# Gated linear attention and routed experts: squares summed on the matrix engine, masks ahead of key copies, and a re-timed instruction order

## The chip, the cores and the metric

The kernel runs on one core of a Trainium2 chip. A core has engines that run side by side, each through a queue of its own: TensorE multiplies matrices (PE in the profile; PEld is its loading of weights), VectorE (DVE) and ScalarE (ACT) work element by element, GpSimd (POOL) and SyncE (SP) mostly issue transfers here. TensorE writes into PSUM, eight banks of 512 fp32 columns on 128 partitions; the other data lie in SBUF. The metric is the time of one execution on the device, in microseconds.

## What is computed

The reference has two stages. The first is an attention with a complex gate per key dimension; the gate's size is limited to 0.999 first:

```python
B, H, S, D = 4, 8, 768, 48
mag = np.sqrt(a_re * a_re + a_im * a_im)
scale = np.minimum(mag, 0.999) / (mag + 1e-06)
a_re_n, a_im_n = (a_re * scale, a_im * scale)
for t in range(S):
    new_re = ar * S_re - ai * S_im          # ar, ai: gates of step t
    new_im = ar * S_im + ai * S_re
    kv = np.einsum('bhd,bhe->bhde', k[:, :, t], v[:, :, t])
    S_re, S_im = (new_re + kv, new_im)
    y[:, :, t] = np.einsum('bhd,bhde->bhe', q[:, :, t], S_re)
```

Its output, 3072 rows of 384, goes into eight experts. Each row takes the expert with the largest logit:

```python
logits = x @ w_gate                          # (3072, 8)
expert_idx = np.argmax(logits, axis=1)       # gate_w: softmax weight of that expert
xe = x[mask]                                 # rows of expert e
h = np.maximum(xe @ w1[e], 0.0)              # 384 -> 1024
out[mask] = gate_w[mask, None] * (h @ w2[e]) # 1024 -> 384
```

## The kernel before

The recurrence is written as a product of gates. For each of the four batches the kernel goes through these steps:

- **limit**: the gates of 16 steps lie in four tiles of 4 steps by 144 columns (576 columns of 128 partitions each, real and imaginary). Each is scaled by a function of the sum of its squares.
- **front** and **fix**: running complex products of gates, on VectorE.
- **fold**: the running products are multiplied into the queries, and their inverses into the keys. The inverse needs a sum of squares again, of 768 columns. Transfers then bring the rows into tiles KX and QX of one head each.
- **attention**: for each chunk of 128 steps and each pair of heads: score product, causal mask, output product, and the state that is carried on.

The batches overlap. Every step is recorded as an operation with an engine, a duration and a latency. A scheduler in the kernel itself orders the list by these guessed times, and then each engine's instructions are issued in that order. [...]

```python
def dve(cols, emit, after=(), free=(), first=5):
    return op("V", cols / 960 + 0.068, cols / 960 + 0.19, emit, after, free, first)
def act(cols, emit, after=(), free=(), first=5, n=1):
    return op("A", n * 0.08 + cols / 1200, n * 0.08 + cols / 1200 + 0.15, emit, after, free, first)
def pe(passes, emit, after=(), free=(), first=5):
    return op("T", passes * 0.111, passes * 0.111 + 0.21, emit, after, free, first)
def dma(late, emit, after=(), free=()):
    return op("S", 0.62, late, emit, after, free)
...
for o in in_time(ops):       # the scheduler's order
    o.emit()
```

The limit, with the sum of squares on VectorE (vstt is a three-operand instruction, vtt a two-operand one):

```python
sq = act(2 * n, ... A.activation(sq2, g[:, :, 1:3, :], func=ACT.Square))          # 1152 columns
o = dve(n, ... vstt(s, sq2[:, :, 0, :], 1e-12, sq2[:, :, 1, :], ALU.max, ALU.add), [sq])
ln = act(n, ... A.activation(l, s, func=ACT.Ln), [o])
ex = act(n, ... A.activation(l, l, func=ACT.Exp, scale=-0.5), [ln])
uu = act(n, ... A.activation(u, l, func=ACT.Square, accum_out=good[...]), [ex])
o = dve(n, ... vtt(s, s, u, ALU.mult), [uu])
o = dve(n, ... vstt(l, s, -3.0, l, ALU.add, ALU.mult), [o])
uu = act(n, ... A.activation(u, l, func=ACT.Identity, scale=..., bias=w_bias), [o])
sc = dve(n, ... vstt(s, l, -2 / 0.999, u, ALU.max, ALU.mult), [uu])
o = dve(2 * n, ... )                                                              # gates times s
```

Attention. The diagonals hold the end of a chunk on the diagonal of a matrix, so that a score product yields the state's decay as well; two ScalarE instructions make one for a head and a chunk:

```python
ats = [... for p in ps[0:4]]                    # score banks, used in turn
for c in range(C - 1):
    for i in range(n):
        def diagonal(i=i, c=c):
            for w in range(2):
                A.activation(QX[i][0:R2, c, 128 + w * D:...], diag[:, w, :], func=ACT.Copy,
                             scale=KX[i][0:R2, c * CW + 128 + w:...])
        turn[c, i] = act(96, diagonal, of(kd[i], c), ...)
for c in range(C):
    for j, r in enumerate(units):               # a unit is a pair of heads
        o = pe(6.8 if c < C - 1 else 4, score, ...)                # 4 products of 224 columns
        needs = [dve(256, ... vtt(ak[:, :, 0:128], at[:, :, 0:128], causal, ALU.mult), [o], ak_readers, first=0)]
        if c < C - 1:
            needs.append(act(2 * R2, ... A.copy(ak[:, :, 128:], at[:, :, 128:128 + R2]), [o], ak_readers, first=1))
        o = pe(..., outputs, needs + ...)
        e = act(wide, ... ys from the output bank ..., [o])
        ...                                     # two transposes, state copy, row copy, logits
```

The experts run when all rows have been scattered by expert in DRAM. Their products take turns over three sets of banks:

```python
own = {"x": (6, 7), "h": (2, 3, 4, 5), "o": (0, 1)}[kind]
```

Of the kernel before, what the change touches and what calls it, by code (L numbers as in the profile page):

```python
# [9 lines left out]
FP32 = mybir.dt.float32  # L10
# [127 lines left out]
def gateloop_then_moe(ctx, tc, q, k, a_re, a_im, v, wg, w1, w2, out):  # L138
# [58 lines left out]
    w_bias = consts.tile([128, 1], FP32, name="w_bias")  # L197
    nc.vector.memset(w_bias, -0.4995)
# [60 lines left out]
    ps = [bank.tile([128, 512], FP32, name=f"bank{i}") for i in range(8)]  # L259

    with ExitStack() as att:
# [15 lines left out]
        lsq, fsq = part(1, JQ, 2, NC), part(1, BL, 2, C * NB)  # L277
# [31 lines left out]
        ats = [p.rearrange("p (h w) -> p h w", w=256) for p in ps[0:4]]  # L309
# [11 lines left out]
        def op(engine, busy, late, emit, after=(), free=(), first=0):  # L321
            ops.append(Op(engine, busy, late, emit, list(after), list(free), first))
            return ops[-1]
# [7 lines left out]
        def pe(passes, emit, after=(), free=(), first=5):  # L331
            return op("T", passes * 0.111, passes * 0.111 + 0.21, emit, after, free, first)

        def dma(late, emit, after=(), free=()):
            return op("S", 0.62, late, emit, after, free)
# [20 lines left out]
        def load_gates(b, tiles):  # L356
            cs = columns(tiles)
            for i in range(BL // JQ):
                js = slice(i * JQ, i * JQ + JQ)
                old = sum((state.pop(("gate", i, t), []) for t in tiles), [])  # L360
                raw = [dma(7.5, lambda p=p, src=src, i=i, js=js: Q.dma_start(gates[i][:, :, p, cs], src[b, :, js, cs]),
                           free=old) for p, src in ((1, a_re), (2, a_im))]
                for t in tiles:
                    state["raw", i, t] = raw

        def limit(b, tiles):

            cs = columns(tiles)
            wide = len(tiles) * TC
            for i in range(BL // JQ):  # L370
                w, readers = ring("lim", 2)
                s, l, u = (x[:, :, cs] for x in lim[w])
                g = gates[i][:, :, :, cs]
                sq2 = lsq[:, :, :, cs]
                n = JQ * wide
                sum_at = NG + b * (BL // JQ) + i
                sq = act(2 * n, lambda g=g, sq2=sq2: A.activation(sq2, g[:, :, 1:3, :], func=ACT.Square), state["raw", i, tiles[0]],
                         state.get("lsq", []))
                o = dve(n, lambda s=s, sq2=sq2: vstt(s, sq2[:, :, 0, :], 1e-12, sq2[:, :, 1, :], ALU.max, ALU.add), [sq], readers)
                state["lsq"] = [o]  # L380
                ln = act(n, lambda s=s, l=l: A.activation(l, s, func=ACT.Ln), [o], readers)
                ex = act(n, lambda l=l: A.activation(l, l, func=ACT.Exp, scale=-0.5), [ln])
                uu = act(n, lambda l=l, u=u, at=sum_at: A.activation(u, l, func=ACT.Square, accum_out=good[:, at:at + 1]), [ex], readers)
                state.setdefault("good", []).append(uu)

                o = dve(n, lambda s=s, u=u: vtt(s, s, u, ALU.mult), [uu])
                o = dve(n, lambda s=s, l=l: vstt(l, s, -3.0, l, ALU.add, ALU.mult), [o])
                uu = act(n, lambda l=l, u=u: A.activation(u, l, func=ACT.Identity, scale=-0.5e-6 * 0.4995, bias=w_bias), [o])
                sc = dve(n, lambda s=s, l=l, u=u: vstt(s, l, -2 / 0.999, u, ALU.max, ALU.mult), [uu])
                o = dve(2 * n, lambda g=g, s=s: vtt(g[:, :, 1:3, :], g[:, :, 1:3, :], bc(s[:, :, None, :], [128, JQ, 2, wide]), ALU.mult),  # L390
                        [sc])
                taken_by(readers, o)
                m = act(n, lambda g=g: A.activation(g[:, :, 0, :], g[:, :, 2, :], func=ACT.Copy, scale=-1.0), [o])
                for t in tiles:
                    state["scaled", i, t] = [o, m]

        def front(b, tiles):
# [6 lines left out]
            for j in range(1, BL):  # L404
                g, r = gates[j // JQ], j % JQ
                w = j % 2
                z = zs[w][:, :, :, 0:n]
                at = dims(g[:, r - 1], 2 * NC + cs.start, (-NC, 2), (0, 2), (1, n)) if j == 1 else                     dims(X[:, j - 1], NC + cs.start, (-NC, 2), (0, 2), (1, n))
                m = dve(4 * n, lambda z=z, g=g, r=r, at=at: vtt(z, dims(g[:, r], cs.start, (NC, 2), (NC, 2), (1, n)), at, ALU.mult),
                        state["scaled", j // JQ, tiles[0]] + [o], state.get(("z", w), []))  # L410
                if j == 1:
                    c0 = act(2 * n, lambda g=g: A.copy(X[:, 0, :, cs], g[:, 0, 1:3, cs]), state["scaled", 0, tiles[0]], old)
                o = dve(2 * n, lambda z=z, j=j: vtt(X[:, j, :, cs], z[:, 0], z[:, 1], ALU.add), [m], old)
                state["z", w] = [o]
                steps.append(o)
                for t in tiles:
                    state.setdefault(("gate", j // JQ, t), []).extend([m, c0] if j == 1 else [m])
# [63 lines left out]
        def fold_chunks(b, t, chunks, fixed, lq, lk, packed, free, old, new):  # L481
# [6 lines left out]
            f2, s, l = fsq[:, :, :, at], fs[:, :, at], fl[:, :, at]  # L488
            by_chunk = lambda ap: ap.rearrange("p j (c n) -> p c j n", n=NB)
# [5 lines left out]
            sq = act(2 * n, lambda: A.activation(f2, x, func=ACT.Square), there, old["fsq"])  # L495
            o = dve(n, lambda: vstt(s, f2[:, :, 0, :], LEAST / 1e8, f2[:, :, 1, :], ALU.max, ALU.add), [sq], old["fs"])
            state["fsq"].append(o)

            ln = act(n, lambda: A.activation(l, s, func=ACT.Ln), [o], old["fl"])
# [4 lines left out]
                                                     in0=s[:, BL - 1].rearrange("p (n b) -> p n b", b=NB)[:, :, NB - 1],  # L504
# [10 lines left out]
            o = dve(n, lambda: vtt(s, s, l, ALU.mult), [ex], [g])  # L515
# [20 lines left out]
        def attention(b, g):  # L536
# [16 lines left out]
            for c in range(C - 1):  # L553
                for i in range(n):
                    def diagonal(i=i, c=c):
                        for w in range(2):
                            A.activation(QX[i][0:R2, c, 128 + w * D:128 + w * D + D], diag[:, w, :], func=ACT.Copy,
                                         scale=KX[i][0:R2, c * CW + 128 + w:c * CW + 129 + w])
                    turn[c, i] = act(96, diagonal, of(kd[i], c), state.get(("head", slots[i]), []), first=2, n=4.6)
            st = [None for _ in units]  # L560
            for c in range(C):
                wide = 128 + (R2 if c < C - 1 else 0)
                for j, r in enumerate(units):
                    (w, readers), (wa, ak_readers), (wy, y_readers), (ws, s_readers) = ring("at", 4), ring("ak", 3), ring("yst", 4), ring("ys", 3)
# [8 lines left out]
                    o = pe(6.8 if c < C - 1 else 4, score, sum((of(qd[i], c) + of(kd[i], c) + [turn.get((c, i))] for i in r), []), readers,  # L573
# [3 lines left out]
                    if c < C - 1:  # L577
                        needs.append(act(2 * R2, lambda at=at, ak=ak: A.copy(ak[:, :, 128:], at[:, :, 128:128 + R2]), [o], ak_readers, first=1))
# [9 lines left out]
                    o = pe((4.2 if c == 0 else 7.6) * wide / 224, outputs, needs + [state["vb"][c]] + ([old[1]] if old else []), y_readers,  # L588
# [13 lines left out]
                    if c < C - 1:  # L602
                        (wp, p_readers), (wt, t_readers) = ring("st_ps", 2), ring("st", 4)
                        o = pe(1, lambda wp=wp, ys=ys: T.transpose(st_ps[wp][0:R2, :], ys[:, 128:128 + R2], ident), [e], p_readers, first=rank)
# [6 lines left out]
                    o = pe(1, lambda wp=wp, ys=ys: T.transpose(y_ps[wp], ys[:, 0:128], ident), [e], p_readers, first=rank)  # L611
# [7 lines left out]
                    o = pe(2, lambda c=c, ys=ys, pair=pair: T.matmul(lg_ps[b % 2][:, c, :, pair], lhsT=ys[:, 0:128], rhs=wgate[:, pair, :],  # L619
# [93 lines left out]
        limited = [((0, 1, 2),)] * 4  # L713
        multiplied = [((0, 1, 2),)] * 3 + [((0, 1), (2,))]
        pieces = lambda b, t: ((0, 3), (3, C)) if (b, t) == (B - 1, G - 1) else ((0, C),)
        for b in range(B):
            for tiles in limited[b]:
                load_gates(b, tiles)
            to_limit = list(limited[b])
            for tiles in multiplied[b]:  # L720
                while to_limit and to_limit[0][0] <= tiles[-1]:
                    limit(b, to_limit.pop(0))
# [11 lines left out]
                for t, f in zip(tiles, fixed):  # L734
                    fold(b, t, f)
                    attention(b, t)

# [17 lines left out]
    with ExitStack() as ms:  # L755
# [33 lines left out]
        def bank_of(kind):  # L789
            own = {"x": (6, 7), "h": (2, 3, 4, 5), "o": (0, 1)}[kind]  # L790
            turn[kind] = turn.get(kind, -1) + 1
            return ps[own[turn[kind] % len(own)]]
# [273 lines left out]
```

## Time and profile before

| what | value |
|---|---|
| time, median of three runs | 695.32 us (694.79 to 696.25) |
| span of the profiled execution | 693.6 us |
| TensorE busy | 518.6 us (75%) |
| VectorE busy | 373.5 us (54%) |
| ScalarE busy | 295.5 us (43%) |
| mean granted TensorE clock | 0.93 |

Most of the kernel's instructions are issued by one helper, so nearly all groups carry its line, L134; they are told apart by operation, by the tiles that they write and read, and by shape. "out<-in" names these tiles, without buffer numbers: "big" are the large buffers that hold gates, squares and running products in the attention and the weights in the expert stage, "ak" is the masked score tile, "bank" is PSUM. Behind the bar stand the group's busy time in us, the mean ns of one instruction, and the idle time of the engine just before them with what ended it. In a timeline the columns are the start in us, the duration, the engine, the instruction, how many in a row, and in brackets the idle time of that engine before it.

An average over the span says little here, since the attention and the experts have different limits; each must be read by itself.

### The profile page before, as it was taken

What the parts mean: (1) busy time and instruction counts of PE and PEld (TensorE: products, weight loads), DVE (VectorE), ACT (ScalarE), POOL (GpSimd) and SP (SyncE); (2) the same over time, 40 slices, a digit from 0 to 9 for tenths busy, and PEclk for the clock granted to TensorE, in tenths of its full rate; (3) what the DMA queues carried; (4) which work ended last, traced back from release to release, by engine and by line L of the source; (5) the groups of instructions that cost most, each with busy time, mean ns of one, the idle gap of its engine ahead of it and who ended that gap; (6) DMA issues with size and microseconds to landing.
All of it is one profiled execution on the core that took longest, in us unless ns stands there. A gap on an engine that the chain in (4) does not pass through costs nothing. (4 is left out here: it accounts for less than half of the span.)

```text
span 693.6 us, 8193 instructions
## 1 busy us (share of the span) xinstructions
PE 518.6 (75%) x2590; PEld 324.1 (47%) x2590; DVE 373.5 (54%) x776; ACT 295.5 (43%) x980; POOL 72.8 (10%) x90
## 2 busy tenths in 40 slices
PE   0000289806959348698897899999999999999993
PEld 0000166504636236476565665555556565555552
DVE  5999999997997999999714121202020111111010
ACT  6655499937996559578874010100010101010100
POOL 8000000000021000400212101020201010111101
PEclk9999999956978669799999799999999999999997
DMA  8130779789632291638449746646465569300000
GB/s 250 35 99 4 183 186 255 195 177 208 182 114 93 62 228 42 183 99 216 126 128 423 234 84 232 169 133 162 135 165 174 151 173 221 82 17 23 9 11 29
DMA packets 75747, 98.68 MB, mean 142 GB/s; under 512 B 10397, under 2 KB 65455, under 8 KB 73648
## 3 DMA queue, kind: packets, MB, share of 16 engines
q1 hardware_dynamic: 70800, 78.97, 44.7%
q0 software_dynamic: 3456, 9.47, 3.8%
q10 hardware_dynamic: 1440, 9.65, 3.6%
q8 instruction: 22, 0.36, 0.3%
q14 instruction: 29, 0.24, 0.1%
HBM read 64.04 MB, written 15.78 MB: 115 GB/s over the span
## 5 line engine op out<-in xcount | busy, mean ns | idle before, releaser
L134 PE MATMUL bank<-QX,KX 128*128 128x224 f32 (+1 forms) x384 | 95.1, 380 | 124.1 <-ACT QX L134 100.6
L134 PE MATMUL bank<-big,ht 128*128 128x384 f32 (+1 forms) x624 | 142.0, 422 | 0.0
L134 PE MATMUL bank<-xt,big 128*128 128x448 f32 (+1 forms) x384 | 141.3, 528 | 0.0
L134 PEld LDWEIGHTS bank<-QX,KX 128*128 128x128 f32 x384 | 70.2, 210 | 140.0 <-issue 91.3
L134 PEld LDWEIGHTS bank<-big,ht 128*128 128x128 f32 (+1 forms) x624 | 87.8, 169 | 55.6 <-issue 6.9
L134 PEld LDWEIGHTS bank<-xt,big 128*128 128x128 f32 x384 | 72.5, 191 | 65.3 <-issue 61.6
L134 ACT ACTIVATE QX<-diag,KX 96x48 f32<-96x48 f32 x320 | 83.7, 330 | 14.5 <-DMA KX<-pk 14.3
L134 ACT ACTIVATE big<-big 128x576 f32<-128x576 f32 (+3 forms) x93 | 79.4, 864 | 20.7 <-DVE big L134 19.0
L865 DVE TENSOR_SCALAR ht<-bank 128x448 f32<-128x448 f32 (+1 forms) x32 | 19.5, 608 | 121.0 <-PE bank L134 121.0
L867 ACT ACTIVATE ht<-bank 128x448 f32<-128x448 f32 (+1 forms) x32 | 17.0, 530 | 125.9 <-PE bank L134 125.9
L134 DVE TENSOR_TENSOR big<-big,big 128x576 f32<-128x576 f32 (+3 forms) x86 | 65.1, 767 | 0.4
L134 PE MATMUL bank<-ident,ys 128*128 128x128 f32 (+1 forms) x176 | 47.6, 309 | 23.3 <-ACT xf L134 9.4
L134 DVE TENSOR_TENSOR big<-big 128x288 f32<-128x288 f32 (+5 forms) x120 | 63.4, 543 | 1.1 <-ACT big L134 0.6
L696 POOL DMA_INDIRECT sorted_x<-xf,slot x24 | 27.3, 1136 | 340.4 <-DVE ak L134 177.6
L134 PE MATMUL bank<-ak,vb 128*48 128x224 f32 (+1 forms) x384 | 55.7, 371 | 6.7 <-DVE ak L134 5.4
L878 ACT ACTIVATE yo<-bank,gt 128x384 f32<-128x384 f32 x14 | 8.1, 581 | 116.6 <-PE bank L134 116.6
L134 DVE TENSOR_TENSOR ak<-bank,causal 128x256 f32<-128x256 f32 x96 | 40.3, 421 | 29.4 <-PE bank L134 15.1
L817 POOL DMA_INDIRECT out_dram<-yo,to x23 | 22.3, 971 | 239.7 <-ACT yo L878 187.7
L134 PEld LDWEIGHTS bank<-ident,ys 128*128 128x128 f32 (+1 forms) x176 | 25.1, 156 | 44.1 <-ACT ys L134 16.0
L134 PE MATMUL bank<-QX,st 128*48 128x224 f32 (+1 forms) x320 | 43.6, 352 | 1.0 <-ACT st L134 0.9
L134 ACT ACTIVATE ys<-bank 128x224 f32<-128x224 f32 (+1 forms) x96 | 31.9, 340 | 16.7 <-PE bank L134 13.4
L134 DVE SCALAR_TENSOR_TENSOR big<-big 128x576 f32<-128x576 f32 x48 | 36.0, 753 | 5.5 <-ACT big L134 5.4
(120 smaller groups left out, 482.9 us busy)
## 6 DMA issues: line engine op xcount, KB each, us to landing
big<-in_moe_w_dram SPq DMA_DIRECT2D x10, 1536.0 KB
xq<-sorted_x SPq DMA_DIRECT2D x28, 504.0 KB
big<-in_moe_w_dram ACTq DMA_DIRECT2D x6, 1536.0 KB
KX<-pk SPq DMA_DIRECT2D x44, 146.2 KB
QX<-pk SPq DMA_DIRECT2D x44, 144.0 KB
sorted_x<-empty SPq DMA_DIRECT2D x8, 675.5 KB
big<-in_a_re_dram SPq DMA_DIRECT2D x16, 288.0 KB
big<-in_a_im_dram SPq DMA_DIRECT2D x16, 288.0 KB
```

The costliest lines, as they stand in the source:

```text
L134: return lambda *a, **kw: self.tc.keep_in_program_order(f(*a, **kw))
L696: move = nc.gpsimd.indirect_dma_start(out=sorted_x[:, :], out_offset=bass.IndirectOffsetOnAxis(ap=slot[:, i:i + 1], axis=0), in_=xfs[(b * ...
L817: move = nc.gpsimd.indirect_dma_start(out=rows, out_offset=bass.IndirectOffsetOnAxis(ap=index, axis=0), in_=y, in_offset=None, bounds_chec ...
L865: nc.vector.tensor_scalar_max(ht[:, f, cols], h, 0.0)
L867: nc.scalar.activation(ht[:, f, cols], h, func=ACT.Relu)
L878: nc.scalar.activation(y, o, func=ACT.Copy, scale=gt[:, i, 0:1])
```

## The change

It has six parts, most of them in the attention:

- **Squares by identity products.** In the limits of batches 1 to 3, and in the last two of the four of batch 0, the two squares are summed by products with the identity matrix that accumulate in PSUM. Two banks become one tile, "two", for these sums. The small constant that kept the logarithm from zero becomes the logarithm's bias, read from a tile. The same form is there for the fold, switched off; its sum becomes a two-operand addition.
- **Score banks.** As banks 0 and 1 hold the sums, the scores take turns over two banks and not four.
- **Masks first.** In the list, the key copy comes after the mask.
- **Durations.** Products and transfers are listed with longer latencies, and some products with longer durations. The limits of the next batch are recorded among the attentions of the one at hand.
- **Diagonals of the last group** are made by VectorE, all heads' chunks of a piece with one instruction per head.
- **Banks of the experts.** Transposes and results trade banks.

The aim is less work and less waiting on VectorE in the attention. The diff, cut to its core (cuts are marked with "..."):

```diff
-    ps = [bank.tile([128, 512], FP32, name=f"bank{i}") for i in range(8)]
+    two = bank.tile([128, 1024], FP32, name="two")
+    ps = [two[:, 0:512], two[:, 512:]] + [bank.tile([128, 512], FP32, name=f"bank{i}") for i in range(2, 8)]
...
-        ats = [p.rearrange("p (h w) -> p h w", w=256) for p in ps[0:4]]
+        ats = [p.rearrange("p (h w) -> p h w", w=256) for p in ps[2:4]]
...
-            return op("T", passes * 0.111, passes * 0.111 + 0.21, emit, after, free, first)
+            return op("T", passes * 0.111, passes * 0.111 + 0.45, emit, after, free, first)
-            return op("S", 0.62, late, emit, after, free)
+            return op("S", 0.62, late + 1.0, emit, after, free)
...
+        def sum_of(squares, sq):
+            flat = squares.rearrange("p u j n -> p u (j n)")
+            n = flat.shape[2]
+            def add():
+                for a, z in ((0, 512), (512, n)):
+                    for u in range(2):
+                        T.matmul(two[:, a:z], lhsT=ident, rhs=flat[:, u, a:z], start=(u == 0), stop=(u == 1))
+            o = pe(n * 4 / 1200 / 0.111 + 0.8, add, [sq], state.get("sum", []))
+            return two[:, 0:n].rearrange("p (j n) -> p j n", j=squares.shape[2]), o
...
-                o = dve(n, lambda s=s, sq2=sq2: vstt(s, sq2[:, :, 0, :], 1e-12, sq2[:, :, 1, :], ALU.max, ALU.add), [sq], readers)
+            by_pe = b > 0 or i > 1
...
+            if by_pe:
+                s2, o = sum_of(lsq, sq)
+            else:
+                s2 = s
+                o = dve(n, lambda s=s, sq2=sq2: vtt(s, sq2[:, 0], sq2[:, 1], ALU.add), [sq], readers)
-                ln = act(n, lambda s=s, l=l: A.activation(l, s, func=ACT.Ln), [o], readers)
+            ln = act(n, lambda s2=s2, l=l: A.activation(l, s2, func=ACT.Ln, bias=w_bias[:, 2:3]), [o], readers)
...
+            by_pe = len(pieces(b, t)) == 1 and (False)                       # in the fold
-            o = dve(n, lambda: vstt(s, f2[:, :, 0, :], LEAST / 1e8, f2[:, :, 1, :], ALU.max, ALU.add), [sq], old["fs"])
+                o = dve(n, lambda: vtt(s, f2[:, 0], f2[:, 1], ALU.add), [sq], old["fs"])
...
+            late = (b, g) == (B - 1, G - 1)
+            for c0, c1 in pieces(b, g) if late else ():
+                for i in range(n):
+                    m = min(c1, C - 1) - c0
+                    o = dve(m * R2, lambda i=i, c0=c0, m=m: vtt(QX[i][...], bc(diag[...]), bc(KX[i][...]), ALU.mult),
+                            of(kd[i], c0), state.get(("head", slots[i]), []), first=2)
...
-            for c in range(C - 1):
+            for c in range(0 if late else C - 1):
...
-                    o = pe(6.8 if c < C - 1 else 4, score, ...
+                    o = pe(7.6 if c < C - 1 else 4.5, score, ...
-                        needs.append(act(2 * R2, ... A.copy(ak[:, :, 128:], at[:, :, 128:128 + R2]), [o], ak_readers, first=1))
+                        needs.append(act(2 * R2, ... A.copy(ak[:, :, 128:], at[:, :, 128:128 + R2]), [o], needs + ak_readers, first=1))
...
+        load_gates(0)
+        for i in range(BL // JQ):
+            limit(0, i)
         for b in range(B):
...
                     attention(b, t)
+                    if b + 1 < B:
+                        if t == 0:
+                            load_gates(b + 1)
+                        for i in ((0,), (1, 2), (3,))[t]:
+                            limit(b + 1, i)
...
-            own = {"x": (6, 7), "h": (2, 3, 4, 5), "o": (0, 1)}[kind]
+            own = {"x": (0, 1), "h": (2, 3, 4, 5), "o": (6, 7)}[kind]
```

## The prediction

> **What bounds the kernel now.** I began with the page's busy tenths, the span in 40 slices of 17.3 us.
>
> ```profile
> PE   0000289806959348698897899999999999999993
> DVE  5999999997997999999714121202020111111010
> ACT  6655499937996559578874010100010101010100
> PEclk9999999956978669799999799999999999999997
> ```
>
> There are two kernels in one. In the first twenty slices (to about 345 us) VectorE is at nine tenths nearly everywhere, and TensorE comes and goes. In the last seventeen TensorE is full and nothing else matters. The change hardly touches the second half, so the question is how much sooner the first ends. The table of busy time in stretches of 15 us says how full VectorE is: added up from 15 to 345 us it is 311.5 us busy out of 330, so some 18 us are idle.
>
> Next I asked what VectorE waits for between 8 and 345 us (us in total, times, longest).
>
> ```profile
> DVE ak L134 <- ACT ak L134: 11.0, 14, 2.3
> DVE big L134 <- ACT big L134: 4.2, 3, 2.3
> DVE fs L134 <- ACT big L134: 2.8, 2, 2.3
> ```
>
> The largest is odd. The causal mask reads one part of a score bank and writes the left columns of ak; the key copy reads the bank's other part and writes the right columns. Neither needs the other, yet the mask waits for the copy. The timeline shows how it costs time.
>
> ```profile
> 161.88 2.72 PE L134 MATMUL bank<-QX,KX 128*128 128x224 f32 x6 [0.71 <-ACT QX L134]
> 162.15 1.90 ACT L134 ACTIVATE QX<-diag,KX 96x48 f32<-96x48 f32 x8
> 163.95 0.30 ACT L134 COPY ak<-bank 128x192 f32<-128x192 f32 x1
> 164.28 0.42 DVE L134 TENSOR_TENSOR ak<-bank,causal 128x256 f32<-128x256 f32 x1 [1.90 <-ACT ak L134]
> ```
>
> Scores come, ScalarE is busy with eight diagonals, then makes the copy, and VectorE, the engine with no time to spare, starts its mask only 0.03 us after the copy's end.
>
> Last I took the groups, with shapes kept apart, for the price of what is added and removed.
>
> ```profile
> L134 DVE SCALAR_TENSOR_TENSOR big<-big 128x576 f32<-128x576 f32 x48 | 36.0, 753 | 5.5 <-ACT big L134 5.4
> L134 DVE TENSOR_TENSOR big<-big 128x576 f32<-128x576 f32 x19 | 14.3, 753 | 0.7 <-ACT big L134 0.6
> L134 ACT ACTIVATE QX<-diag,KX 96x48 f32<-96x48 f32 x320 | 83.7, 330 | 14.5 <-DMA KX<-pk 14.3
> L134 ACT ACTIVATE big<-big 128x576 f32<-128x576 f32 x64 | 43.8, 686 | 11.5 <-DVE big L134 11.2
> L134 ACT ACTIVATE big<-big,w_bias 128x576 f32<-128x576 f32 x16 | 12.4, 777 | 9.3 <-DVE big L134 9.2
> 15.95 1.42 DVE L134 SCALAR_TENSOR_TENSOR big<-big 128x576 f32<-128x576 f32 x2
> ```
>
> The second row has the same 753 ns as the first: three-operand and two-operand forms cost alike. The last line, from the timeline, shows that two in a row take 1.42 us, so each holds VectorE for 0.67 us, not 0.753: durations overlap, and what is saved must be counted by the spacing.
>
> [...] wherever I looked, mask and copy of one bank never overlap (164.28 after 164.25). [...]
>
> **The change part by part.**
>
> *Squares by identity products.* Each of the 16 limits (4 per batch) had one sum of squares on VectorE. Fourteen go to TensorE, two stay as a plain add of the same cost. VectorE is relieved of 14 x 0.67 = 9.4 us. The two of batch 0 lie at the start, where VectorE waits for ScalarE anyway, so I count 12 x 0.67 = 8.0 and half of the other two, 8.7 us. The multiply behind it now reads PSUM; the mask, which reads PSUM too, takes 421 ns for 256 columns, between 353 for 192 and 453 for 288 from SBUF, so no surcharge. TensorE gets 14 sums of 2 x 576 = 1152 streamed columns. Four score products of 224 columns take about 0.92 us, so one sum is 0.92 x 1152/896 = 1.2 us, double at half clock: 17 to 33 us on an engine which, between 75 and 345 us, sums to 191 us busy out of 270. It fits; the extra latency in the limit's chain lies beside other VectorE work. ScalarE pays 0.09 us for a bias pointer in each logarithm, 29 x 0.09 = 2.6 us.
>
> *Fold.* Its switch for the product is off, so 13 three-operand sums become 13 adds, 954 against 953 ns: nothing.
>
> *Masks first.* The scheduling list now puts the copy behind the mask, so the bank's dependency falls the other way and the 11.0 us of VectorE waiting for the copy cannot occur as such. Not all is gain: at 215.02 us the wait was 2.27 us but the copy itself began only at 214.68, as the product was late, so the order is worth 0.34 of it. At 221.27 it is about 0.4 of 1.12, at 164.28 about 1.3 of 1.90. These three give some 2 of 5.3 us; in proportion, 4 of 11.
>
> *New durations.* The list now takes products as 0.24 us later and transfers as 1 us later. It will place other VectorE work ahead of a mask whose score is late, which should win back part of the other 7 us and of the 2.8 us of waits for a fold's squares (held up at 161 us behind diagonals that waited for a transfer). I take 2 to 3 us.
>
> *Two score banks instead of four.* The third score product waits for the mask and the copy of the first. One unit's round on TensorE is about 3 us, mask plus copy 0.75 us, so two suffice in the steady state, but a late mask now reaches TensorE sooner. I charge 1 us, and 1 more for ScalarE sitting behind masks.
>
> *Diagonals of the last group on VectorE.* Forty ScalarE instructions at 0.25 us spacing (eight take 2.00 us at 347.52) are 10 us off ScalarE. Eight VectorE multiplies of 288 or 192 columns, 4 x (0.453 + 0.353) = 3.2 us, come on an engine that is busy 2.64 of 15 us there. But TensorE is busy 13.59 and 13.26 of 15 in the stretches from 345 to 375, so the tail can shrink by little: 1 us.
>
> *Expert results in other banks.* Products, waits and order stay as they are; the expert stage starts when the last scatter has landed (VectorE waits 8.9 us for it until 391.27). Zero.
>
> Sum: 8.7 + 4 + 2.5 + 1 - 2 = 14.2 us. As not all VectorE time becomes end time, I take off a tenth: 12.8 us, or 695.3 - 12.8 = 682.5 us.
>
> **The rivals.** *First, another engine becomes the bound.* From 90 to 135 us VectorE (about 14.5 of 15), TensorE (14.0) and ScalarE (14.3) are all full. Taking VectorE work away there while adding to TensorE and making ScalarE wait for masks could gain nothing or push attention back. If that holds through all batches, the gain shrinks to the order of the mask and the tail, about 4 us: 691. Against it: TensorE has 22.07 us of idle at 160 us waiting for keys, which would absorb a lag. *Second, the waits move.* Fewer score banks and a scheduling list rebuilt from new durations make new stalls on VectorE as large as those removed; the result would be the squares less 9, near 695, or above at worst 700. Against it: the durations are more cautious than before. *Third, the better case:* nearly all 18 us of idle vanish with the squares, 8.7 + 14 + 2 = 25, or 670.
>
> **Range and chances.** The middle is 682.5. The threshold for 2% is 681.4, just beside it, so the two outcomes are close to even. The first rival and part of the second give the upper end of 693, the third nearly the lower of 671. Chances: faster by over 2% 0.45, within 2% 0.48, slower by over 2% 0.07.
>
> **What would show each step.** Right: the group of 48 three-operand instructions at 576 columns falls to 32; sum products appear in the bank called two at about 1.2 to 2.4 us each; "DVE ak <- ACT ak" is gone and VectorE's idle between 15 and 330 us is about 11 us; the last fold product ends near 331 us instead of 344.2; diagonal activations fall from 320 to 280. From the last fold product to the end the distance stays within 1 or 2 us. Wrong: VectorE's busy time falls by about 9 us but its idle grows, with masks waiting for TensorE; or ScalarE's waits for masks grow from 4.7 us to well over 10 and TensorE's with them; or the distance from the last fold to the first expert product grows.

## The result and the profile after

The changed kernel takes 676.81 us (median of four runs, 676.25 to 677.95) against 695.79 us for the kernel before on the same chip: a ratio of 0.9726, 95% interval 0.970 to 0.9752. That is 19 us, where 12.8 were predicted; the time lies inside the range of 671 to 693.

The busy tenths of the changed kernel, in slices of 16.9 us:

```profile
PE   1550379988988478988997999999999999999993
DVE  6999999999999999999633120201020201120010
ACT  6555597869997778767743101000010001000100
PEclk9666599979899678989998899999999999999997
```

VectorE now stands at nine tenths without a break from the second slice to the nineteenth, where before two slices of that stretch stood at seven. TensorE works in the first slices too: these are the identity products, at a granted clock of five to six tenths.

VectorE's largest waits between 8 and 330 us (us in total, times, longest), as the last fold now ends at 333 us:

```profile
DVE big L134 <- ACT big L134: 5.1, 8, 2.4
DVE ak L134 <- PE bank L134: 1.5, 3, 1.2
DVE fs L134 <- ACT big L134: 1.5, 1, 1.5
```

The 11.0 us behind key copies are gone. A mask waits for its scores alone, 1.5 us in all. The mirror image has grown: ScalarE's copies wait for masks. Over the whole span these waits are, in the kernel before and then in the changed one,

```profile
ACT ak L134 <- DVE ak L134: 4.7, 7, 1.9
```

```profile
ACT ak L134 <- DVE ak L134: 10.3, 17, 1.7
```

The groups of the changed kernel that answer to those shown before:

```profile
L134 DVE SCALAR_TENSOR_TENSOR big<-big 128x576 f32<-128x576 f32 x32 | 24.2, 755 | 1.2 <-ACT big L134 1.2
L134 DVE TENSOR_TENSOR big<-two,big 128x576 f32<-128x576 f32 x14 | 10.5, 752 | 0.5 <-ACT big L134 0.3
L134 PE MATMUL two<-big,ident 128*128 128x512 f32 x56 | 39.4, 842 | 36.1 <-ACT big L134 25.9 <-DVE big L134 9.9
L134 ACT ACTIVATE QX<-diag,KX 96x48 f32<-96x48 f32 x280 | 71.6, 331 | 8.9 <-DMA KX<-pk 8.8
```

Three-operand instructions fell from 48 to 32, diagonals from 320 to 280, and a multiply that reads PSUM takes 752 ns, where one of the same size from SBUF takes 754. To see what this is worth, I cut the stretch that VectorE governs out of both traces: from 15 us to the end of the last fold's key products, at 344.20 us before and 332.96 after. The columns are the stretch, its length, and busy us of TensorE, its weight loads, VectorE, ScalarE and GpSimd with their instructions, then the granted clock, the share of the transfer engines and GB/s. First before, then after:

```profile
15.00:344.20 329.20, 190.34 (x1293) 130.30 (x1295) 311.52 (x604) 239.01 (x823) 18.32 (x20) 0.89 0.56 141
```

```profile
15.00:332.96 317.96, 234.75 (x1395) 153.74 (x1395) 306.48 (x594) 238.54 (x812) 21.75 (x24) 0.84 0.58 149
```

VectorE's busy time fell by 5.0 us and its idle time from 17.7 to 11.5, by 6.2: together 11.2 us. The span of the two profiled executions fell by 17.3, so 6.1 us came after the last fold. Here is where, in the timeline of before: TensorE's products for an early tile of the first expert's rows, the last scatter's issue, the first instruction that had waited for its landing, and the first main product of the experts.

```profile
382.13 7.14 PE L134 MATMUL bank<-big,big 128*128 128x128 f32 x48
382.57 0.97 POOL L696 DMA_INDIRECT sorted_x<-xf,slot  x1 [0.30 <-issue]
391.27 0.15 DVE L831 CAST to_e<-big 128x1 int32<-128x1 f32 x1 [8.88 <-DMA sorted_x<-xf,slot]
400.95 7.27 PE L134 MATMUL bank<-xt,big 128*128 128x320 f32 x26
```

And in the changed kernel:

```profile
366.02 8.57 PE L134 MATMUL bank<-big,big 128*128 128x128 f32 x48
366.92 0.97 POOL L729 DMA_INDIRECT sorted_x<-xf,slot  x1 [0.30 <-issue]
370.46 0.15 DVE L867 CAST to_e<-big 128x1 int32<-128x1 f32 x1 [4.18 <-DMA sorted_x<-xf,slot]
382.64 5.63 PE L134 MATMUL bank<-xt,big 128*128 128x320 f32 x14
```

| stretch of the path | before, us | after, us | gain |
|---|---|---|---|
| start to the last fold's end | 344.2 | 333.0 | 11.2 |
| to the last scatter's issue | 38.4 | 34.0 | 4.4 |
| to its landing | 8.7 | 3.5 | 5.2 |
| to the experts' first main product | 9.7 | 12.2 | -2.5 |
| to the end | 292.7 | 293.7 | -1.0 |

Landing 5.2 us sooner was in no term of the prediction, nor were the 2.5 us lost behind it. The first line of each view tells part of that loss. Before, TensorE was through with these early products at 389.27 us, 2.0 us before the first instruction behind the landing; now they end at 374.59 us, 4.1 us after it, so the landing no longer holds the path and not all of its 5.2 us could be gained. From the scatter's issue to the first main product the gain is 2.7 us (18.4 to 15.7). The experiments had to settle three things: what each part is worth, why the scatter lands sooner, and why the experts' start is slower.

### The profile page after: what moved, and what is told of

Read it like the earlier page. It is cut to its first block, busy times and chain, and to the rows that moved or that the text cites. A ratio compares the mean times of both kernels' runs of the same rounds, so it can differ in the third digit from the quotient of the medians.

```text
span 676.3 us, 8400 instructions
## 1 busy us (share of the span) xinstructions
PE 562.9 (83%) x2702; PEld 348.3 (52%) x2702; DVE 370.6 (55%) x772; ACT 289.8 (43%) x940; POOL 72.4 (11%) x90
## 5 line engine op out<-in xcount | busy, mean ns | idle before, releaser
L134 PE MATMUL bank<-xt,big 128*128 128x448 f32 (+1 forms) x384 | 142.9, 533 | 0.0
L134 PEld LDWEIGHTS bank<-QX,KX 128*128 128x128 f32 x384 | 67.8, 204 | 54.9 <-issue 35.8
L134 PE MATMUL two<-big,ident 128*128 128x512 f32 (+1 forms) x112 | 46.0, 568 | 36.1 <-ACT big L134 25.9
L134 ACT ACTIVATE QX<-diag,KX 96x48 f32<-96x48 f32 x280 | 71.6, 331 | 8.9 <-DMA KX<-pk 8.8
L134 ACT ACTIVATE big<-big 128x576 f32<-128x576 f32 (+3 forms) x77 | 68.6, 904 | 14.6 <-DVE big L134 12.9
L134 PE MATMUL bank<-ident,ys 128*96 128x128 f32 (+1 forms) x176 | 47.3, 306 | 17.3 <-ACT ys L134 7.0
L134 DVE TENSOR_TENSOR big<-big 128x288 f32<-128x288 f32 (+5 forms) x108 | 55.3, 519 | 6.1 <-ACT big L134 5.2
L134 PEld LDWEIGHTS two<-big,ident 128*128 128x128 f32 x112 | 23.7, 245 | 59.2 <-issue 34.6
L134 PEld LDWEIGHTS bank<-ident,ys 128*96 128x96 f32 (+1 forms) x176 | 26.0, 157 | 31.8 <-ACT ys L134 13.1
## 6 DMA issues: line engine op xcount, KB each, us to landing
xq<-sorted_x SPq DMA_DIRECT2D x28, 504.0 KB, 11.2
```

The costliest lines, as they stand in the source:

```text
L134: return lambda *a, **kw: self.tc.keep_in_program_order(f(*a, **kw))
```

## The experiments

The scheduler makes one caution necessary. Any edit of the list gives another order of hundreds of instructions, with waits of its own. So three of the runs are controls that move one guessed number by next to nothing. In three runs (the old durations in the changed kernel, the second control of it, and that of the kernel before) the new order changed some of the output's values, by a dependence between instructions that I did not trace; they hold the same instructions, and I use their times only for how much an order can matter, and rest no part's worth on them. One part of the change was varied by no run: the limits of the next batch, recorded among the attentions of the one at hand, are in every version of the changed kernel and in none of the kernel before.

In the table, idle and busy are VectorE's from 15 us to the last fold's end; "gap" is from the issue of the last weight fetch during the attention to the issue of the last scatter, "landing" from there to its landing, in us.

| run | ratio to before (95%) | busy | idle | gap | landing |
|---|---|---|---|---|---|
| kernel before | 1 | 311.5 | 17.7 | 16.3 | 8.7 |
| changed kernel | 0.9726 (0.970 to 0.9752) | 306.5 | 11.5 | 22.8 | 3.5 |
| changed, control 1 | 0.9774 (0.9733 to 0.9815) | 304.8 | 14.7 | 22.7 | 3.6 |
| changed, control 2 | 0.9753 (0.9704 to 0.9803) | 306.6 | 14.1 | 20.9 | 5.3 |
| before, control | 1.0074 (1.0045 to 1.0102) | 313.1 | 23.8 | 14.7 | 9.6 |
| changed, no identity products | 0.9802 (0.9754 to 0.9851) | 311.7 | 10.5 | 22.1 | 4.5 |
| changed, copy free of mask | 0.9826 (0.9791 to 0.9862) | 305.5 | 17.0 | 21.9 | 3.7 |
| changed, old durations | 0.9890 (0.9848 to 0.9932) | 305.9 | 23.4 | 18.9 | 5.8 |
| changed, diagonals on ScalarE | 0.9790 (0.9756 to 0.9824) | 304.5 | 17.0 | 20.5 | 4.4 |
| before, new durations | 0.9880 (0.9836 to 0.9923) | 312.0 | 13.7 | 18.7 | 9.2 |
| before, masks first and new durations | 0.9842 (0.9795 to 0.989) | 312.4 | 9.2 | 19.7 | 6.9 |
| before, fetch ahead in the list | 1.000 (0.9986 to 1.0015) | 311.6 | 17.2 | 16.3 | 8.9 |
| before, weights of two experts | 0.9928 (0.9899 to 0.9956) | 311.9 | 17.8 | 17.9 | 3.5 |
| changed, transposes in banks 7 and 0 | 0.9707 (0.9673 to 0.9741) | 306.5 | 13.1 | 21.9 | 4.7 |

**The controls.**

```diff
-            return op("T", passes * 0.111, passes * 0.111 + 0.45, ...     # changed kernel, control 1
+            return op("T", passes * 0.111, passes * 0.111 + 0.44, ...
-            return op("S", 0.62, late + 1.0, ...                          # changed kernel, control 2
+            return op("S", 0.62, late + 1.05, ...
-            return op("T", passes * 0.111, passes * 0.111 + 0.21, ...     # kernel before
+            return op("T", passes * 0.111, passes * 0.111 + 0.22, ...
```

> A control: the changed kernel with one guessed number moved by nothing that matters, a product's latency in the list from 0.45 to 0.44 us. The scheduler gives another order of the same instructions. Theory 1, the four parts act by their mechanisms and the order between them is worth little: within 1.5 us of the changed kernel, ratio to before 0.971 to 0.975. Rival, the changed kernel's order is also a lucky one among many: 3 us slower or more, ratio 0.977 or above, and then the first runs' losses of 4 to 7 us for each single part hold some 3 us that belong to no part.

> The same control by another number: transfers listed 1.05 and not 1.0 us later. Theory 1: ratio 0.971 to 0.975. Rival, a lucky order: 0.977 or above.

> The control for the kernel before: a product's latency in the list 0.22 and not 0.21 us. Theory 1: within 1.5 us of the kernel before, ratio 0.998 to 1.002. Rival, the kernel before has a lucky order of its own: 3 us slower or more, 1.004 or above; were it faster by as much, the change's gain would hold some luck of that kind.

One hundredth of a microsecond in the list costs the kernel before 0.0074 (some 5 us). The changed one loses 0.0048 (some 3 us) to the first control and 0.0027 to the second, but both intervals overlap with its own. VectorE's idle time rises with it, by 6.1 us before and by 3.2 and 2.6 us after. The rival has it for the kernel before; for the changed one these runs lean that way. Besides, the changed kernel and the last run of the table have the same order in the attention, and their idle times differ by 1.6 us. A single part must therefore be judged against 0.975 to 0.977 as much as against 0.9726, and a difference of a few us in time alone shows nothing; waits and busy times tell more.

**No identity products.**

```diff
-            by_pe = b > 0 or i > 1
+            by_pe = False
```

> The changed kernel with all sums of squares of the limits on VectorE as two-operand additions (no identity products; two score banks, masks first, new durations and the rest stay). Theory 1, VectorE's work sets the end of the attention: 14 additions of 0.67 us come back, of which the two of batch 0 count half, so about 8.7 us more than the changed kernel's 676.8: 685, with the last fold's key products some 8 to 9 us later. Rival, the products cost TensorE and ScalarE about what VectorE is spared: within 2 us of 676.8.

0.9802, or 5.3 us more than the changed kernel (0.0076 of 695.8) and 2 to 3 us more than its controls, whose intervals overlap with it. Between the two theories, then. The last fold ends 4.2 us later (337.17 against 332.96 us), not 8 to 9. VectorE's busy time tells it better: 311.7 against 306.5 with the products, 5.2 us and not 8.7. Here chance is small: all seven kernels without the products have 311.5 to 313.1 us, all seven with them 304.5 to 306.6, so this run lies 5.1 to 7.2 us above the latter. The durations of VectorE's instructions in the stretch, counted one by one, fall by 8.0 us between these two kernels (355.2 to 347.2), but they overlap by 43.5 us in the one and 40.8 in the other: some of what is taken out had been hidden behind a neighbour. Why the rest overlaps less stays open.

**Copy free of the mask.**

```diff
-  ... A.copy(ak[:, :, 128:], at[:, :, 128:128 + R2]), [o], needs + ak_readers, first=1))
+  ... A.copy(ak[:, :, 128:], at[:, :, 128:128 + R2]), [o], ak_readers, first=1))
```

> The changed kernel with the key copy no longer listed behind the mask; all else stays. Theory 1: the order of the two is worth about 4 us, so 681, and VectorE's waits for key copies return with several us in total. Rival, the new durations alone keep masks from waiting, whatever the order: 677, with under 2 us of VectorE waiting for copies.

0.9826, 7 us more than the changed kernel and 4 to 5 more than the controls, with which its interval overlaps. VectorE's largest waits from 8 to 330 us in this run:

```profile
DVE ak L134 <- ACT ak L134: 7.2, 8, 1.7
DVE big L134 <- ACT big L134: 4.2, 6, 2.4
```

With the list's order gone the old wait is back, 7.2 us of it (the kernel before has 11.0, its control 6.4), and idle time is 17.0 us against 11.5 to 14.7 in the changed kernel and its controls. Idle time alone would not be proof (the run with the diagonals back, below, has as much); the name of the wait is. This is theory 1, by its mechanism: in the changed kernel the new durations alone do not keep masks from waiting. ScalarE's waits for masks over the whole span are 13.6 us in this run, more than the 10.3 of the changed kernel, so it is not the order alone that makes them.

**Durations.** In the changed kernel the old numbers, in the kernel before the new ones (the same lines, the other way):

```diff
-            return op("T", passes * 0.111, passes * 0.111 + 0.45, ...
+            return op("T", passes * 0.111, passes * 0.111 + 0.21, ...
-            return op("S", 0.62, late + 1.0, ...
+            return op("S", 0.62, late, ...
-                    o = pe(7.6 if c < C - 1 else 4.5, score, ...
+                    o = pe(6.8 if c < C - 1 else 4, score, ...
...                  # outputs 4.8 and 8.4 to 4.2 and 7.6, transposes 1.5 to 1, logits 2.5 to 2
```

> The changed kernel with the old latencies and durations of products and transfers in the list; all else stays. Theory 1: the durations are worth 2 to 3 us, so 679. Rival, they are what removed most of VectorE's waits: 684 or more, with VectorE's waits for TensorE and ScalarE between 8 and 330 us growing from about 19 us to over 25.

> The kernel before with the new latencies and durations of products and transfers in its list, and nothing else of the change. The prediction's term: 2 to 3 us, ratio 0.996. Rival, from the changed kernel with the old durations: these numbers are the largest part, VectorE's idle time between 15 us and the last fold falls from 17.7 to below 14 us, and the ratio is 0.988 or less. Chance orders are worth some 5 us either way, as the controls showed.

In the kernel before, the new numbers alone give 0.988, or 8.3 us. Idle time falls from 17.7 to 13.7 us, and the waits for key copies to 3.3 us without any change of order between mask and copy:

```profile
DVE big L134 <- ACT big L134: 3.7, 3, 1.8
DVE ak L134 <- ACT ak L134: 3.3, 9, 0.6
DVE ak L134 <- PE bank L134: 2.4, 3, 1.2
```

Masks placed later in VectorE's queue found their scores, and often the copy as well, already done: 2.4 and 3.3 us of waits are left. The marks of the rival came true, and in time alone these numbers are the largest part, three times what was predicted: the interval (5.3 to 11.4 us) excludes 2.5, though not the 5 us that an order can be worth by chance. But VectorE's waits are less than half of it. The profiled execution is 9.3 us shorter than that of before: the last fold ends 3.5 us sooner (340.67 us), and 4.5 of the other 5.7 us lie between the last fold and the last scatter (33.8 and not 38.4 us). That distance moves with the order: the control of the kernel before, with the old numbers, has 34.2 us, and the first control of the changed kernel, with the new ones, 37.6. What the numbers won where the prediction sought it is the 4.0 us of idle time. The old numbers in the changed kernel point the same way, with 23.4 us idle; its output differs, so nothing rests on it. (Its expectation starts from about 19 us of waits, which is the figure of the kernel before; between 8 and 330 us the changed kernel has 11.6, and this run 21.2.)

**Masks first and durations together**, on the kernel before:

> The kernel before with masks first and the new durations together; four score banks, squares and diagonals as before. Theory: these two make up most of the fall of idle time; VectorE's idle time comes to 11 to 15 us as in the changed kernel and its controls, its busy time stays at 311 to 312 us, its waits for key copies vanish, and the ratio is about 0.987. Rival, they need the squares on TensorE as well: idle time stays above 16 us and the ratio above 0.993.

0.9842: 11 us of 19, with squares, diagonals and banks as they were. The four runs spread from 679.6 to 686.1 us, and the fastest is the profiled one. The key copies' wait is gone from the list:

```profile
DVE big L134 <- ACT big L134: 5.3, 5, 2.0
DVE fs L134 <- ACT fl L134: 1.5, 2, 1.0
DVE pk L134 <- issue: 1.2, 1, 1.2
DVE ak L134 <- PE bank L134: 1.0, 2, 0.7
```

Idle time is 9.2 us, the lowest of all runs and below the 11 to 15 expected; busy time stayed at 312.4. So the fall of idle time needs nothing from the squares. Two score banks do not stand in its way either: the run without identity products has two, and 10.5 us.

**Diagonals back on ScalarE**, in the changed kernel:

```diff
-            late = (b, g) == (B - 1, G - 1)
+            late = False
```

> The changed kernel with the last group's diagonals back on ScalarE. Theory 1, as the prediction had it: worth 1 us in the tail, so 678. Rival, from the trace of the changed kernel: the diagonals kept ScalarE from issuing the fetch of the first experts' weights, which then stood in front of the last scatters; the fetch goes back by some 5 us against the first score of the last group, the last scatter lands about 8 us after its issue and not 3.5, and the time is 680 to 682.

0.9790, within the intervals of the controls: no worth in time can be shown. The landing took 4.4 us, not 8, so the rival of this run falls as it was stated. The gap in the table shows what holds. With the new durations it is 18.7 to 20.5 us where ScalarE makes the diagonals (three runs) and 20.9 to 22.8 where VectorE does (six runs). With the old ones it is 14.7 to 16.3 us in three runs and 18.9 in the one with VectorE's diagonals. Both parts move the fetch forward against the last scatter, each by 2 to 4 us in the mean.

**Fetch and landing.** The first try only raised the fetch's priority:

```diff
-            op("A", 1.3, 20.0, lambda e=e: fetch(e, A), state["last heads"], wait, 5)
+            op("A", 1.3, 20.0, lambda e=e: fetch(e, A), state["last heads"], wait, -1)
```

> The kernel before with the fetch of the first experts' weights put ahead of diagonals in the list (its priority only); the diagonals stay on ScalarE. Theory of the fetch: it is issued several us sooner against the first score of the last group, the weights are through before the last scatters, which land in 3 to 5 us and not 8, and the time falls by 2 to 4 us. Rival, the landing was slow for another reason: it stays near 8 us and the time within 1 us of before.

The gap did not move (16.3 us): in the list the fetch is ready only when the last heads' keys have been transferred, and in the trace it still follows the last diagonals, so nothing was tried. The second removed work from in front of the scatter: the third expert's weights are fetched after the first loads of rows, and the order on the engines stays.

```diff
-            op("A", 1.3, 20.0, lambda e=e: fetch(e, A), ...
+            op("A", 1.3, 20.0, lambda e=e: fetch(e, A) if e < 2 else None, ...
                 xq, gt_next = load(e + 1)
+                if e == 0:
+                    fetch(2, IQ)          # queue of the row loads, kept in order behind them
```

> The kernel before with only the weights of two experts fetched during the attention, those of the third behind the first loads of rows; the order on TensorE, VectorE and ScalarE stays, but for the two missing fetches. Theory, 9.4 MB of weights stand in front of the last scatters: with 6.3 MB the last scatter lands 3.5 to 5 us after its issue and not 8.7, the first main product of the experts comes 3 to 4 us sooner after the last scatter's issue than the 18.4 us of before, and the ratio is about 0.995. Rival, the weights have nothing to do with it: landing still 8 us or more, ratio 0.999 to 1.001.

```profile
380.78 0.97 POOL L696 DMA_INDIRECT sorted_x<-xf,slot  x1 [0.31 <-issue]
384.26 0.15 DVE L831 CAST to_e<-big 128x1 int32<-128x1 f32 x1 [4.07 <-DMA sorted_x<-xf,slot]
...
395.16 2.15 PE L134 MATMUL bank<-xt,big 128*128 128x320 f32 x7
```

The scatter lands 3.5 us after its issue, not 8.7, the first main product follows the last scatter's issue by 14.4 us and not 18.4, and the kernel before becomes 0.9928 of itself, 5 us faster. (The issue itself also comes 1.8 us sooner; why was not tried.) The theory holds. The table says the same without it: gap and landing add up to 24.4 to 27.9 us in all thirteen kernels that fetch three experts' weights, and to 21.4 in the one that fetches two. And where a trace records both landings, it shows the weights go first. The kernel before with the new durations, its last weight fetch and its last scatter (KB each, then us from issue to landing):

```profile
big<-in_moe_w_dram ACTq DMA_DIRECT2D x1, 1536.0 KB, 25.8
sorted_x<-xf,slot POOLq DMA_INDIRECT x1, 8.3
```

The fetch was issued at 355.80 us and landed at 381.6, the scatter at 374.51 and 382.8. In all seven traces with three experts' weights that record both, the scatter is issued before the weights have landed and lands 1.2 to 2.7 us after them. With two experts' weights these land at 378.9, before the scatter's issue, and the scatter takes 2.6 us by its own record. In these runs, then, the last scatter landed within 4 us of its issue only where the fetch was issued 21.9 us or more ahead of it (3.5 to 3.7 us), or brought the weights of two experts (3.5 us).

**Transposes in banks 7 and 0**, in the changed kernel:

```diff
-            own = {"x": (0, 1), "h": (2, 3, 4, 5), "o": (6, 7)}[kind]
+            own = {"x": (7, 0), "h": (2, 3, 4, 5), "o": (6, 7)}[kind]
```

> The changed kernel with the first rows' transposes in banks 7 and 0 instead of 0 and 1, so that two of them never share the tile of two banks. Theory, transposes wait for copies because the two banks are one tile: from the first of them to the first main product of the experts 1.8 to 2.0 us and not 3.05, and the time 1.2 us less, ratio about 0.971. Rival, the gaps lie in the order: still 3 us, ratio 0.9726.

The changed kernel's first transposes of rows, and then those of this run:

```profile
379.59 0.58 PE L134 MATMUL two<-ident,xs 128*128 128x128 f32 x3
380.87 0.64 PE L134 MATMUL two<-ident,xs 128*128 128x128 f32 x3 [0.69 <-DVE xt L842]
382.02 0.69 PE L134 MATMUL two<-ident,xs 128*128 128x128 f32 x3 [0.52 <-ACT xt L840]
```

```profile
379.13 0.59 PE L134 MATMUL bank<-ident,xs 128*128 128x128 f32 x3
379.65 0.64 PE L134 MATMUL two<-ident,xs 128*128 128x128 f32 x3
380.32 0.43 ACT L840 COPY xt<-two 128x320 f32<-128x320 f32 x1 [2.98 <-PE two L134]
380.40 0.64 PE L134 MATMUL bank<-ident,xs 128*128 128x128 f32 x3
380.98 13.19 PE L134 MATMUL bank<-xt,big 128*128 128x320 f32 x48
```

Two banks that are one tile to the program were guarded as one here: each group of transposes waited for the copy of the group before (0.69 and 0.52 us), though it wrote the other bank. Kept apart they run through, 1.85 us from the first transpose to the main products where it was 3.05. The other runs agree: 3.00 us in the six other versions of the changed kernel, 1.84 or 1.85 in all six of the kernel before. The run takes 674.15 us, 0.9707 of before, the best version of all; the times of the two versions alone (intervals overlap) would not show the 1.2 us, the timeline does.

## Why the prediction was right, and where its steps were off

The middle of 682.5 was 6 us too high, and the kind of gain was right: VectorE's work and waits in the attention. For the attention alone it was close: the last fold was to end near 331 us, and ended at 333.0. The rest of the gain came from behind the last fold, for reasons that it did not name; that was luck.

- **What bounds the kernel**: right. The last fold's end and the end of the kernel moved together, and the expert stage kept its length within 1 us.
- **Squares, 8.7 us**: right in mechanism, mis-sized. Busy time fell by 5.0 us, by 5.2 against the run without the products. The spacing of two instructions in a row was taken for the worth of each; overlap was lost with them. In time the part lies between nothing and 5 us, and no run here parts it from chance order. The bias's price on ScalarE was right where the two kernels compare directly: the fold's logarithm of 768 columns takes 936 ns with the bias from a tile and took 844 without. The products' price on TensorE was underrated, too: 44 us of busy time in the stretch and not 17 to 33. ("Half clock" is the granted 0.50 of the kernel before in the stretches 150 to 165 and 240 to 255 us.) The slip is in "four score products of 224 columns take about 0.92 us". The kernel makes two products there, one for each head of a pair, and the trace holds two records for each (384 records for 192 score products in all). So 0.92 us is the time of 448 columns, and a sum of 1152 takes 0.92 x 1152/448 = 2.4 us. The trace has a sum, four products in eight records, at granted clocks of 0.50 and then 1.00:

```profile
22.19 4.53 PE L134 MATMUL two<-big,ident 128*128 128x512 f32 x8 [4.33 <-DVE big L134]
164.27 2.27 PE L134 MATMUL two<-big,ident 128*128 128x512 f32 x8
```

- **Room on TensorE**: right. It took these products and VectorE's idle time did not grow.
- **Masks first, 4 us, and durations, 2 to 3 us**: the sum of 6.5 fits the 6.2 us by which idle time fell. Put into the kernel before, one on top of the other, the durations take idle time from 17.7 to 13.7 us and masks first to 9.2: 4.0 and 4.5 us. That is not far from the split, but a chance order alone moved idle time by up to 6.1 us. In time the split does not show: durations alone are worth 8.3 us, more than half of it behind the last fold, and masks first adds 0.0038 to them, within both intervals, while taking it from the changed kernel brings 7.2 us of waits back. The two parts attack the same waits, so their single worths need not add up. No run shows what ties mask and copy of one bank together; the runs show that the wait goes with the list (VectorE's waits for copies: 11.0 us before, none in the changed kernel, 7.2 with the copy free of the mask).
- **Two score banks, -2 us**: ScalarE's waits for masks grew from 4.7 to 10.3 us, as feared, yet VectorE's idle time did not. How much of this is the banks' is not parted: with four banks, masks first and the new durations it is 8.0 us.
- **Tail, 1 us, "from the last fold product to the end the distance stays within 1 or 2 us"**: this step failed. The distance fell by 6.1 us. The last scatter landed 5.2 us sooner after its issue, of which 2.7 us were left at the first main product. Its landing was taken as fixed ("the expert stage starts when the last scatter has landed") without asking what held it for 8.7 us: 9.4 MB of weights. The 4.4 us between fold and scatter are not assigned to a part; over all the runs that distance is 33 to 38 us.
- **Banks of the experts, zero**: 1.2 us lost, by the tile of two banks. A further 1.3 us or so to the first main product lies in TensorE's early products, which took 8.57 us at a granted clock of 0.64 where before they took 7.14 at 0.78. Over the fourteen traces these same products take 5.62 us at 1.00, 7.14 to 7.25 at 0.76 to 0.78, 7.82 at 0.70, and 8.12 to 8.57 at 0.64 to 0.68. Why the clock was lower is open. The 1.0 us after the first main product came with a lower clock too (0.94 from 384 to 400 us, against 1.00 from 402 to 418 us of the kernel before); no run tried that.
- **Rivals**: the first (another engine becomes the bound) and the second (waits move) did not come true. The third, better case asked for nearly all idle time to vanish; a third of it did.

## What to carry to other kernels

Where a kernel's order is made from guessed durations, the guesses are a tuning part of their own: longer latencies in the list took 4.0 us of idle time from the full engine here without any change to its work. A single order holds luck, so measure a nudged twin before crediting a part with a few microseconds. And look at how long every transfer on the path takes to land: a bulk fetch issued some 15 to 23 us ahead of a small transfer set the small one's time here, and putting off a third of that fetch gave 5 us to the kernel before without touching the attention.

## What the runs showed of the hardware

Two things were unexpected. An identity product of 512 fp32 columns stands in the trace as two records, each of about 0.59 us at a granted clock of 1.00 and 1.10 us at 0.50 (842 ns in the mean of all). The four sums between 22 and 52 us have TensorE to themselves, 4.2 to 4.5 us long and one every 8 to 9 us; the granted clock was 0.50 to 0.55 within each of them, and 0.57 in the mean of the stretch. And a small scatter of rows landed 1.2 to 2.7 us after bulk loads issued before it, in all seven traces of three experts' weights that record both. Thirteen kernels agree within 3.5 us on when the last scatter lands after the last bulk fetch is issued (24.4 to 27.9 us), though the gap between the two issues ranges from 14.7 to 22.8 us.
